# A new order for the weight sums, high parts and low parts of the second MLP product, and a fourth buffer for its raw weights

## The chip, the core and the metric

The kernel runs on one core of one Trainium2 chip. The metric is the device time of one execution in microseconds (us). The engines that matter here are TensorE (PE in the profile, with its weight loads listed as PEld), VectorE (DVE), ScalarE (ACT), GpSimd (POOL) and SyncE (SP). In this part of the kernel POOL and SP only issue transfers. Each engine takes its instructions in the order in which they stand in its queue; engines wait for each other through semaphores.

## The reference

The block is a linear-attention layer followed by an MLP over the tokens. Only the second half of the MLP is touched here:

```python
def _B_ref(x, w1, b1, w2, b2):
    h = _layernorm(x, axis=-1)                       # (B, S, D)
    u = jnp.einsum("bsd,sf->bdf", h, w1) + b1        # (B, D, F)
    u = _gelu(u)
    y = jnp.einsum("bdf,fs->bds", u, w2) + b2        # (B, D, S)
    return y.transpose(0, 2, 1)

x = A_x
h = x + _A_ref(_layernorm(x, axis=-1), A_wqkv, A_w_phi, A_wo)
h2 = h + _B_ref(_layernorm(h, axis=-1), B_w1, B_b1, B_w2, B_b2)
```

S = 2048 tokens, D = 512 channels, F = 1792 hidden units, everything in float32. The second product is `y = u @ w2`, with 1792 x 2048 weights.

## The kernel before

The kernel has four parts that overlap at their edges: projections of the attention, its output with the second layer norm, the first MLP product (weights w1, until about 386 us of the span), and the second MLP product (weights w2, from there to the end). The change is in the last part.

Float32 accuracy is reached by splitting every operand into a high part in the format float32r and a low part, which is the difference; a product is then high x high, high x low and low x high. To save products, the second MLP product goes over 2 x 2 blocks of the matrices and uses seven products of sums of blocks in place of eight (the scheme of Strassen and Winograd). The seven operands on the weights' side are w2's four blocks, of which one is overwritten by a sum, and three more sums; they lie in one raw tile of 7 x 256 columns (`wraw`), so that one instruction makes all seven high parts (`whi`, on ScalarE) and one all seven low parts (`wlo`, on VectorE).

The work is cut thus. The output has 16 tiles of 128 tokens, taken as 8 row pairs (`sp` 0 to 7). A row pair needs all 14 tiles of hidden units, taken as 7 pairs (`p` 0 to 6). One (sp, p) is a step, n = 7 sp + p; there are 56. Weights are loaded for `GRP` = 2 steps at a time: a group g holds steps 2g and 2g + 1, there are 28 groups (`NGR`), and a load is 512 KB. A group begins in the middle of a row pair when sp is odd, since 7 is odd.

The names used below, with their lines:

- S(g), the sums of group g (`sums_w2`, L773): it starts the load (L771, on SP's queue), makes the sums on VectorE (L782, L783, L784), and before the change also issues the high parts.
- H(g), the high parts: one ACTIVATE of 128 x 1792 on ScalarE (L785) from `wraw` into `whi`, which has 3 buffers, so H(g) waits until TensorE has finished group g - 3.
- L(g), the low parts (`lo_w2`, L787): one VectorE subtraction of 128 x 1792 (L794) into `wlo`, which has 2 buffers, so L(g) waits until TensorE has finished group g - 2. TensorE reads it first at the second matmul of group g (L810).
- The load of group g goes into one of 3 raw buffers, and so waits until L(g - 3) has read the old contents.
- C(sp), the combination at the end of a row pair (L846 to L873): the six PSUM banks of the row pair are put together into two output tiles by VectorE (L855 to L862) with four copies by ScalarE (`e` L852, `low` L854), and four accumulating transfers leave from POOL's queue (L866, L871, L872, L873). The last row pair has its own combination (L878 to L899).
- There are 8 PSUM banks. A row pair takes 6, in turn, so that its third to sixth banks are the ones that held the first to fourth bank of the row pair before; TensorE waits there until C has read them.

The last two steps of a row pair (p = 5 and 6) run as one block, bank by bank. In that block group g's second half is needed one step early when sp is even.

The order of PE, DVE and ACT in this part is the order of the program text (`manual_schedule`, L825); SP's and POOL's queues are ordered by the scheduler. Before the change, S and L are called in this order: ahead of the steps S(0), L(0), S(1); then at each even n with p < 6 one S and one L, S first; and at the end of an even row pair (n even, p = 6) one L between the first and second output tile of C, and one S after C. On VectorE this reads

```
row pair 0:  S2 L1  S3 L2  S4 L3  C0a L4 C0b S5
row pair 1:  S6 L5  S7 L6  S8 L7  C1
row pair 2:  S9 L8  S10 L9  S11 L10  C2a L11 C2b S12
```

and so on. The pool `hp` (L762) is opened on the place where the first product's weight buffers `wf` lay (L517: raw, high and low, four of each); before the change it holds only `hb`, two tiles of the last row pair that are read back from the output (L880).

Of the kernel before, what the change touches and what calls it, by code (L numbers as in the profile page):

```python
# [9 lines left out]
F32 = mybir.dt.float32  # L10
F32R = mybir.dt.float32r  # L11
AF = mybir.ActivationFunctionType
# [5 lines left out]
P = 128  # L18
# [6 lines left out]
GRP = 2  # L25
# [11 lines left out]
def block_kernel(ctx: ExitStack, tc: tile.TileContext, x, xT, wT, phic, wo, w1, b1, w2, b2,  # L37
                 kvmask, ident_in, out):
    nc = tc.nc
# [33 lines left out]
    sums = ps_s.tile([P, SUMS, NPR, 2, 2], F32, name="smq")  # L73
# [26 lines left out]
    def load_x(t):  # L100
        raw = kk.tile([P, KD, P], F32, name="xraw", bufs=3)
        nc.sync.dma_start(raw, xT[t])
        return raw
# [298 lines left out]
    for t in range(3, NT - 1):  # L402
        if t + 2 < NT:
            raw = load_x(t + 2)
# [310 lines left out]
    ws = ctx.enter_context(tc.tile_pool(name="ws", bufs=2, side="right", reuse_waits="tile"))  # L715
# [46 lines left out]
    hp = ctx.enter_context(tc.tile_pool(name="hp", bufs=1, reuse_waits="tile"))  # L762

    STEPS = [(sp, p) for sp in range(NT // 2) for p in range(NP)]
    NGR = len(STEPS) // GRP
    RAW, WH, AW = {}, {}, {}
    done = {"sums": 0, "lo": 0}

    def load_w2(g):
        RAW[g] = ws.tile([P, 7, GRP * P], F32, name="wraw", bufs=3)  # L770
        nc.sync.dma_start(RAW[g][:, 1:5], w2[g])  # L771

    def sums_w2():  # L773

        g = done["sums"]
        if g == NGR:
            return
        done["sums"] += 1
        load_w2(g)
        raw = RAW[g]  # L780
        WH[g] = ws.tile([P, 7, GRP * P], F32R, name="whi", bufs=3)
        nc.vector.tensor_add(raw[:, 0:2], raw[:, 1].unsqueeze(1).to_broadcast([P, 2, GRP * P]), raw[:, 2:4])  # L782
        nc.vector.tensor_add(raw[:, 5], raw[:, 1], raw[:, 2])  # L783
        nc.vector.tensor_add(raw[:, 6], raw[:, 4], raw[:, 5])  # L784
        nc.scalar.activation(WH[g], raw, AF.Copy)  # L785

    def lo_w2():  # L787

        g = done["lo"]
        if g == NGR:  # L790
            return
        done["lo"] += 1
        wl_ = ws.tile([P, 7, GRP * P], F32R, name="wlo", bufs=2)
        nc.vector.tensor_sub(wl_, RAW[g], WH[g])  # L794
        for i, step in enumerate(STEPS[g * GRP:(g + 1) * GRP]):
            AW[step] = WH[g][:, :, i * P:(i + 1) * P], wl_[:, :, i * P:(i + 1) * P]

    with tc.issue_after(LO[-18]), tc.issue_after(LD[-20]):
        sums_w2()
        lo_w2()  # L800
        sums_w2()

    PROD = ((2, 1, 0, None), (5, 5, 1, None), (0, 0, 2, 0), (1, 4, 2, 1), (3, 6, 3, None), (6, 2, 4, None),
            (4, 3, 5, None))
# [11 lines left out]
    def products(sp, ps, order):  # L816
        for a, b, bk, half in order:
            for p in ps:
                wh_, wl_ = AW[sp, p]
                product(bank[bk], half, (wh_[:, a], wl_[:, a]), UB[p, b], half != 1, p == 0, p == NP - 1)  # L820

    def flat(a):
        return a.rearrange("p k d -> p (k d)")
# [3 lines left out]
    for n, (sp, p) in enumerate(STEPS):  # L827
        t = 2 * sp
        last = t + 2 == NT
        if n % GRP == 0 and p < NP - 1:  # L830
            sums_w2()
            lo_w2()
        if p == 0:
            bank = []
            for _ in range(6):
                pool = (ps_f, ps_q, ps_b, ps_b)[n_bank % 8 // 2]
                bank.append(pool.tile([P, 2, HD], F32, name="py", tag="pu"))
                n_bank += 1
        order = LAST if last else PROD
        if p < NP - 2:  # L840
            products(sp, [p], order)
            continue
        if p < NP - 1:
            continue
        products(sp, [p - 1, p], order)
        e = uo.tile([P, 2, HD], F32, name="e")  # L846
        u2 = uo.tile([P, HD], F32, name="u2", bufs=1)
        u3 = uo.tile([P, HD], F32, name="u3")
        if not last:
            ot = uo.tile([P, 2, 2, HD], F32, name="ot", bufs=1)  # L850
            low = uo.tile([P, 3, HD], F32, name="low", bufs=1)
            nc.scalar.activation(e[:, 1], bank[0][:, 0], AF.Copy)  # L852
            for i in range(3):
                nc.scalar.activation(low[:, i], bank[3 + i][:, 1], AF.Copy)  # L854
            nc.vector.tensor_add(e[:, 1], bank[0][:, 1], e[:, 1])  # L855
            nc.vector.tensor_sub(u2, bank[1][:, 0], e[:, 1])
            nc.vector.tensor_add(u2, bank[1][:, 1], u2)
            nc.vector.tensor_sub(u3, u2, bank[2][:, 0])
            nc.vector.scalar_tensor_tensor(e[:, 0], bank[2][:, 1], -1.0, u2, op0=ALU.mult, op1=ALU.subtract)

            def out_block(i, h, o, add):
                nc.vector.scalar_tensor_tensor(ot[:, i, h], o, b2s[:, t + i:t + i + 1], add, op0=ALU.add, op1=ALU.add)  # L862

            out_block(0, 0, bank[2][:, 1], u3)
            out_block(0, 1, bank[3][:, 0], u3)
            nc.gpsimd.dma_start(out[t * P:(t + 1) * P, :], flat(ot[:, 0]), accum_op=ALU.add)  # L866
            if n % GRP == 0:
                lo_w2()
            out_block(1, 0, bank[4][:, 0], e[:, 0])
            out_block(1, 1, bank[5][:, 0], e[:, 1])  # L870
            nc.gpsimd.dma_start(out[(t + 1) * P:(t + 2) * P, :], flat(ot[:, 1]), accum_op=ALU.add)  # L871
            nc.gpsimd.dma_start(out[t * P:(t + 1) * P, HD:D], low[:, 0], accum_op=ALU.add)  # L872
            nc.gpsimd.dma_start(out[(t + 1) * P:(t + 2) * P, :], flat(low[:, 1:3]), accum_op=ALU.add)  # L873
            if n % GRP == 0:
                sums_w2()
            continue

        hb = [hp.tile([P, 2, HD], F32, name=f"hb{i}") for i in range(2)]  # L878
        for i in range(2):
            nc.sync.dma_start(flat(hb[i]), out[(t + i) * P:(t + i + 1) * P, :])  # L880
            nc.vector.tensor_scalar(hb[i], hb[i], b2s[:, t + i:t + i + 1], None, op0=ALU.add)
        nc.scalar.activation(e[:, 1], bank[0][:, 0], AF.Copy)
        nc.vector.tensor_add(e[:, 1], bank[0][:, 1], e[:, 1])
        nc.vector.tensor_add(hb[1][:, 1], e[:, 1], hb[1][:, 1])
        nc.vector.tensor_sub(u2, bank[1][:, 0], e[:, 1])
        nc.vector.tensor_add(u2, bank[1][:, 1], u2)
        nc.vector.tensor_sub(hb[1][:, 0], hb[1][:, 0], u2)
        nc.vector.tensor_sub(u3, u2, bank[2][:, 0])
        nc.vector.tensor_sub(hb[1][:, 0], hb[1][:, 0], bank[2][:, 1])
        nc.vector.tensor_add(hb[0], hb[0], u3.unsqueeze(1).to_broadcast([P, 2, HD]))  # L890
        nc.vector.tensor_add(hb[0][:, 0], bank[2][:, 1], hb[0][:, 0])
        nc.vector.tensor_add(hb[0][:, 1], bank[3][:, 0], hb[0][:, 1])
        nc.vector.tensor_add(hb[0][:, 1], bank[3][:, 1], hb[0][:, 1])
        nc.sync.dma_start(out[t * P:(t + 1) * P, :], flat(hb[0]))
        nc.vector.tensor_add(hb[1][:, 0], bank[4][:, 0], hb[1][:, 0])
        nc.vector.tensor_add(hb[1][:, 0], bank[4][:, 1], hb[1][:, 0])
        nc.scalar.dma_start(out[(t + 1) * P:NT * P, 0:HD], hb[1][:, 0])
        nc.vector.tensor_add(hb[1][:, 1], bank[5][:, 0], hb[1][:, 1])
        nc.sync.dma_start(out[(t + 1) * P:NT * P, HD:D], hb[1][:, 1])  # L899
# [49 lines left out]
```

## Time and profile before

| | |
|---|---|
| time, median of 3 runs | 537.56 us (537.2, 537.56, 539.2) |
| the profiled execution | 539.4 us, of which the span of the profile is 537.6 us |
| granted TensorE clock, mean | 0.999 |
| PE busy in the span | 521.9 us (97%) |
| DVE busy in the span | 394.8 us (73%) |
| ACT busy in the span | 278.4 us (52%) |
| stretch 386.5 to 533.0 us, 146.5 us: PE, DVE, ACT, POOL busy | 142.51, 120.73, 55.86, 24.62 us |

A row of the timeline gives start, duration, engine, line, operation, output <- inputs and shapes, and in brackets the idle time of that engine just before, with what ended it. A row of the waits gives the waiting instruction, what released it, the total in us, how many times, and the longest. The chain of waits is the path of work that ended last, followed back from the end; its rows give start, duration and what. Matmuls overlap in the pipeline, so that a matmul's own duration is longer than the distance to the next one; the distance is what counts.

### The profile page before, as it was taken

The numbers are of one execution on the slowest core, as the hardware profiler recorded it, in microseconds if no ns is written. First come the engines' busy times: TensorE is split into PE (matmuls) and PEld (weight loads), VectorE is DVE, ScalarE is ACT, GpSimd is POOL, SyncE is SP. The second block draws the span as 40 slices with busy tenths as digits, with TensorE's granted clock in tenths as the row PEclk, the third lists the DMA queues.
The fourth block names the chain that finished last, engine by engine and source line by source line (L and its number), as shares of the span: only waits on it lengthen the run. The fifth ranks groups of instructions, "written<-read, shape, count | busy, mean of one in ns | idle before, by whom it ended". The sixth has DMA issues, their size and how long they took to land.

```text
span 537.6 us, 8845 instructions
## 1 busy us (share of the span) xinstructions
PE 521.9 (97%) x3343; PEld 433.8 (81%) x3343; DVE 394.8 (73%) x684; ACT 278.4 (52%) x481; POOL 247.2 (46%) x204
## 2 busy tenths in 40 slices
PE   8999999999999989999999999999999899999996
PEld 7888888886877757778788888888898788888885
DVE  6993999877699989874326426527668878888885
ACT  6998744434337766557755434425534334435330
POOL 2589699876889988886425000000002111211210
PEclk9999999999999999999999999999999999999999
DMA  8534300020502333434333463532027568667752
GB/s 307 191 121 118 98 21 21 1 80 1 159 1 78 99 102 94 119 114 123 98 99 98 117 215 99 177 97 62 20 79 134 127 152 175 139 147 176 146 90 59
DMA packets 36298, 58.52 MB, mean 109 GB/s; under 512 B 3744, under 2 KB 19360, under 8 KB 36256
## 3 DMA queue, kind: packets, MB, share of 16 engines
q1 hardware_dynamic: 31936, 51.37, 30.8%
q0 software_dynamic: 4032, 6.42, 9.5%
q8 instruction: 26, 0.43, 0.4%
q10 hardware_dynamic: 288, 0.17, 0.1%
q14 instruction: 16, 0.13, 0.1%
HBM read 46.81 MB, written 11.14 MB: 108 GB/s over the span
## 4 chain that ended last, share of the span: by engine, by line
PE 57%; DVE 15%; POOL 12%; DMA 6%; ACT 5%; issue 3%; SPq 0%; DVEq 0%; POOLq 0%; ACTq 0%
PE pu L65 10%; PE pu L66 10%; PE pu L67 10%; DMA wraw<-in_w 5%; POOL ez L445 4%; DVE wlo L794 4%; POOL eq L463 3%; PE py L809 3%; PE pv L66 2%; PE pv L67 2%; PE pv L65 2%; PE pk_ps L65 2%; PE pk_ps L66 2%; PE pk_ps L67 2%; PE py L813 2%
## 5 line engine op out<-in xcount | busy, mean ns | idle before, releaser
L66 PE MATMUL pu<-hs,whi 128*128 128x512 f32 x224 | 87.6, 391 | 2.2 <-POOL hs L61 2.2
L604 DVE TENSOR_TENSOR wlo<-wraw,whi 128x512 fp32r<-128x512 f32 x56 | 50.7, 910 | 51.5 <-ACT whi L612 50.4
L65 PE MATMUL pu<-hs,whi 128*128 128x512 f32 x224 | 87.4, 395 | 0.0
L67 PE MATMUL pu<-hs,wlo 128*128 128x512 f32 x224 | 87.0, 390 | 0.0
L866 POOL DMA_DIRECT2D out<-ot x7 | 6.2, 891 | 167.2 <-DVE ot L862 167.2
L785 ACT ACTIVATE whi<-wraw 128x1792 fp32r<-128x1792 f32 x28 | 47.1, 1701 | 62.7 <-DVE wraw L784 53.1
L809 PE MATMUL py<-uf,whi 128*128 128x512 f32 x195 | 71.2, 398 | 0.0
L794 DVE TENSOR_TENSOR wlo<-wraw,whi 128x1792 fp32r<-128x1792 f32 x28 | 56.4, 2021 | 4.5 <-PE py L810 2.2
L612 ACT ACTIVATE whi<-wraw 128x512 fp32r<-128x512 f32 x56 | 34.8, 625 | 46.9 <-PE pu L66 43.2
L810 PE MATMUL py<-uf,wlo 128*128 128x256 f32 x195 | 55.9, 287 | 3.2 <-DVE wlo L794 3.1
L66 PEld LDWEIGHTS pu<-hs,whi 128*128 128x128 f32 x224 | 42.1, 188 | 11.5 <-POOL hs L61 3.2
L65 PEld LDWEIGHTS pu<-hs,whi 128*128 128x128 f32 x224 | 42.1, 188 | 10.8 <-issue 2.5
L67 PEld LDWEIGHTS pu<-hs,wlo 128*128 128x128 f32 x224 | 42.0, 188 | 9.1 <-DVE wlo L604 0.4
L809 PEld LDWEIGHTS py<-uf,whi 128*128 128x128 f32 x195 | 36.8, 189 | 6.9
L445 POOL TENSOR_TENSOR ez<-eq,zB 128x1024 f32<-128x1024 f32 x16 | 40.9, 2561 | 2.5 <-ACT zB L491 2.5
L810 PEld LDWEIGHTS py<-uf,wlo 128*128 128x128 f32 x195 | 36.9, 189 | 6.4 <-DVE wlo L794 6.4
L198 POOL TENSOR_TENSOR pk<-pk,sk 128x1024 f32<-128x1024 f32 x16 | 31.0, 1943 | 9.8 <-DVE sk L197 9.0
L463 POOL TENSOR_TENSOR eq<-eq,w 128x1024 f32<-128x1024 f32 x16 | 32.0, 1998 | 4.0 <-DVE w L460 4.0
L813 PE MATMUL py<-uf,whi 128*128 128x256 f32 x170 | 32.0, 282 | 0.0
L202 POOL TENSOR_TENSOR zacc<-zacc,pk 128x1024 f32<-128x1024 f32 x13 | 31.2, 2401 | 0.6
L809 PE MATMUL py<-un,whi 128*128 128x512 f32 x78 | 29.0, 401 | 0.7 <-DVE ot L862 0.6
L61 POOL TENSOR_TENSOR hs<-hn,hs 128x512 fp32r<-128x512 f32 x16 | 21.5, 1342 | 17.8 <-ACT hs L60 17.8
(183 smaller groups left out, 1319.3 us busy)
## 6 DMA issues: line engine op xcount, KB each, us to landing
wraw<-in_w SPq DMA_DIRECT2D x56, 256.0 KB, 2.8
wraw<-in_w SPq DMA_DIRECT2D x28, 512.0 KB, 4.4
xraw<-in_xT SPq DMA_DIRECT2D x16, 256.0 KB, 3.1
xh<-in_x SPq DMA_DIRECT2D x16, 256.0 KB, 2.7
h<-in_x SPq DMA_DIRECT2D x16, 256.0 KB, 2.8
out<-h SPq DMA_DIRECT2D x16, 256.0 KB, 3.0
out<-ot POOLq DMA_DIRECT2D x14, 256.0 KB, 4.5
wraw<-in_wT SPq DMA_DIRECT2D x12, 256.0 KB, 5.0
```

The costliest lines, as they stand in the source:

```text
L65: nc.tensor.matmul(o, ah, bh, start=first, stop=False)
L66: nc.tensor.matmul(o, ah, bl, start=False, stop=False)
L67: nc.tensor.matmul(o, al, bh, start=False, stop=last)
L445: nc.gpsimd.tensor_mul(EZ[t], EQ[t], zB)
L463: nc.gpsimd.tensor_mul(heads(EQ[t]), heads(EQ[t]), W[t].rearrange("p g c h -> p (g c h)").unsqueeze(2).to_broadcast([P, 2 * H, DH]))
L604: LO.append(nc.vector.tensor_sub(wl_, raw, wh_).ins)
L612: nc.scalar.activation(wh_, raw, AF.Copy)
L785: nc.scalar.activation(WH[g], raw, AF.Copy)
L794: nc.vector.tensor_sub(wl_, RAW[g], WH[g])
L809: nc.tensor.matmul(o, a[0], b, start=start, stop=stop, skip_group_check=True)
L810: nc.tensor.matmul(o[:, 0], a[1], b[:, 0], start=False, stop=stop, skip_group_check=True)
L813: nc.tensor.matmul(o[:, half], a[x], b[:, y], start=start and first and i == 0, stop=stop and i == 2, skip_group_check=True)
```

## The change

The sums, the high parts and the low parts become three functions, called in a new order and with new distances. Ahead of the steps there are now three S, two H and one L. At each even n with p < 6 the order is L, H, S in place of S (with its H), L. In the middle of the combination of an even row pair an H follows the L; the S after it stays. On VectorE this reads

```
row pair 0:  L1 S3  L2 S4  L3 S5  C0a L4 C0b S6
row pair 1:  L5 S7  L6 S8  L7 S9  C1
row pair 2:  L8 S10  L9 S11  L10 S12  C2a L11 C2b S13
```

The raw tiles get names of their own, one buffer each, and a fourth one in the pool `hp`. Groups 0 to 3 use slots 0, 1, 2, 0; from group 4 on the slots go 3, 1, 2, 0 in turn. The load of group g waits from then on for L(g - 4). `hb` lies behind the new buffer in `hp`.

```diff
@@ -764,10 +764,11 @@
     RAW, WH, AW = {}, {}, {}
-    done = {"sums": 0, "lo": 0}
+    done = {"sums": 0, "hi": 0, "lo": 0}
 
     def load_w2(g):
-        RAW[g] = ws.tile([P, 7, GRP * P], F32, name="wraw", bufs=3)
+        slot = g % 3 if g < 4 else (3, 1, 2, 0)[g % 4]
+        RAW[g] = (hp if slot == 3 else ws).tile([P, 7, GRP * P], F32, name=f"wraw{slot}", tag=f"wraw{slot}", bufs=1)
         nc.sync.dma_start(RAW[g][:, 1:5], w2[g])
 
     def sums_w2():
@@ -778,11 +779,18 @@
         done["sums"] += 1
         load_w2(g)
         raw = RAW[g]
-        WH[g] = ws.tile([P, 7, GRP * P], F32R, name="whi", bufs=3)
         nc.vector.tensor_add(raw[:, 0:2], raw[:, 1].unsqueeze(1).to_broadcast([P, 2, GRP * P]), raw[:, 2:4])
         nc.vector.tensor_add(raw[:, 5], raw[:, 1], raw[:, 2])
         nc.vector.tensor_add(raw[:, 6], raw[:, 4], raw[:, 5])
-        nc.scalar.activation(WH[g], raw, AF.Copy)
+
+    def hi_w2():
+
+        g = done["hi"]
+        if g == NGR:
+            return
+        done["hi"] += 1
+        WH[g] = ws.tile([P, 7, GRP * P], F32R, name="whi", bufs=3)
+        nc.scalar.activation(WH[g], RAW[g], AF.Copy)
 
@@ -796,9 +804,12 @@
     with tc.issue_after(LO[-18]), tc.issue_after(LD[-20]):
-        sums_w2()
-        lo_w2()
-        sums_w2()
+        for i in range(3):
+            sums_w2()
+            if i < 2:
+                hi_w2()
+            if i < 1:
+                lo_w2()
 
@@ -828,8 +839,9 @@
         if n % GRP == 0 and p < NP - 1:
+            lo_w2()
+            hi_w2()
             sums_w2()
-            lo_w2()
         if p == 0:
@@ -866,6 +878,7 @@
             if n % GRP == 0:
                 lo_w2()
+                hi_w2()
             out_block(1, 0, bank[4][:, 0], e[:, 0])
```

## The prediction

> **What bounds the kernel now.** I read the page first (TensorE is busy for 97% of the span), then the chain of waits, to see how regularly TensorE advances through the second product, then the table of waits of that stretch, and last the timelines of VectorE, ScalarE and TensorE around the places where it doesn't.
>
> The page's head and its transfers, then the chain of waits (start, duration, what):
>
> ```profile
> span 537.6 us, 8845 instructions
> ...
> out<-ot POOLq DMA_DIRECT2D x14, 256.0 KB, 4.5
> ...
> out<-low POOLq DMA_DIRECT2D x7, 256.0 KB, 6.1
> ```
>
> ```profile
> 387.20 0.72 PE py L813 x6
> ...
> 397.14 0.71 PE py L813 x6
> ...
> 523.61 0.71 PE py L813 x6
> ...
> 529.05 0.44 DVE e L883
> ...
> 534.07 0.42 DVE hb L896
> ```
>
> The six L813 matmuls stand at the same place in every single step. Those of step 0 begin at 387.20, those of step 4 at 397.14: (397.14 - 387.20) / 4 = 2.485 us a step, undisturbed. Those at 523.61 are step 52's. Undisturbed they would come at 387.20 + 52 x 2.485 = 516.42. So TensorE loses 7.19 us in the product, and this is all that an order of the other engines can win there. From 529.05 on the chain is VectorE without a pause, the last combination; it keeps its length.
>
> The waits from 350 us on, and TensorE's timeline at three of the losses:
>
> ```profile
> DVE wraw L782 <- DMA wraw<-in_w: 8.8, 6, 2.9
> PEld py L810 <- DVE wlo L794: 6.4, 10, 1.2
> ...
> PE py L810 <- DVE wlo L794: 3.1, 9, 0.9
> ...
> PEld py L809 <- DVE ot L862: 0.9, 1, 0.9
> ...
> PE py L809 <- DVE ot L862: 0.6, 1, 0.6
> ```
>
> ```profile
> 411.75 0.38 PE L810 MATMUL py<-uf,wlo 128*128 128x256 f32 x1 [0.17 <-DVE wlo L794]
> ...
> 424.55 0.51 PE L809 MATMUL py<-un,whi 128*128 128x512 f32 x1 [0.57 <-DVE ot L862]
> ...
> 429.18 0.39 PE L810 MATMUL py<-uf,wlo 128*128 128x256 f32 x1 [0.91 <-DVE wlo L794]
> ```
>
> Ten times TensorE waits for a late low part, once for a PSUM bank that the combination had not read. (PE and PEld rows of one wait overlap; they aren't added.) Around 424.55, start-to-start distances beyond the normal ones sum to about 1.3 us, which leaves 7.2 - 1.3 = 5.9 us for the ten low parts.
>
> Why they are late, by VectorE's timeline of 396 to 430 us:
>
> ```profile
> 396.54 2.03 DVE L794 TENSOR_TENSOR wlo<-wraw,whi 128x1792 fp32r<-128x1792 f32 x1 [1.50 <-PE py L810]
> ...
> 403.57 2.02 DVE L794 TENSOR_TENSOR wlo<-wraw,whi 128x1792 fp32r<-128x1792 f32 x1 [0.16 <-PE py L810]
> ...
> 406.30 0.68 DVE L782 TENSOR_TENSOR wraw<-wraw 128x512 f32<-128x512 f32 x1
> ...
> 407.82 0.68 DVE L782 TENSOR_TENSOR wraw<-wraw 128x512 f32<-128x512 f32 x1
> ...
> 409.67 2.02 DVE L794 TENSOR_TENSOR wlo<-wraw,whi 128x1792 fp32r<-128x1792 f32 x1 [0.25 <-ACT whi L785]
> ...
> 418.04 0.69 DVE L782 TENSOR_TENSOR wraw<-wraw 128x512 f32<-128x512 f32 x1 [2.89 <-DMA wraw<-in_w]
> ...
> 419.57 2.02 DVE L794 TENSOR_TENSOR wlo<-wraw,whi 128x1792 fp32r<-128x1792 f32 x1
> 421.83 0.42 DVE L855 TENSOR_TENSOR e<-py,e 128x256 f32<-128x256 f32 x1 [0.24 <-ACT e L852]
> ...
> 425.59 0.68 DVE L782 TENSOR_TENSOR wraw<-wraw 128x512 f32<-128x512 f32 x1
> ...
> 427.11 2.02 DVE L794 TENSOR_TENSOR wlo<-wraw,whi 128x1792 fp32r<-128x1792 f32 x1
> 429.04 0.69 DVE L782 TENSOR_TENSOR wraw<-wraw 128x512 f32<-128x512 f32 x1
> ```
>
> From starts: S costs 427.11 - 425.59 = 1.52 us, L 429.04 - 427.11 = 1.93, C 425.59 - 421.83 = 3.76. After row pair 0 two sums (S5 at 406.30, S6 at 407.82) stand ahead of L5, which ends at 411.69; TensorE gets on at 411.75. Before row pair 1's end S8 sits 2.89 us waiting for its load; L7 and C1 are late behind it, the bank is late (424.55), and S9 stands ahead of L8, which ends at 429.13 (TensorE: 429.18). All ten have one of these shapes.
>
> **The change part by part.** *The order on VectorE.* The same instructions run; against the L's, each S moves one place. Two row pairs hold 7 S, 7 L and 2 C, 7 x 3.45 + 2 x 3.76 = 31.7 us, against 14 x 2.485 = 34.8 us of TensorE, so 3.1 us may be idle.
>
> After an even row pair: L4 at 403.57, the rest of C0, S6 from 406.30 to 407.82, then L5 at once, to 409.84: 1.9 us ahead of the 411.75 at which it was taken late, or 1.4 ahead of the 411.3 at which it was wanted. Gain 0.44 there, and the same at its later copies.
>
> At an odd row pair: L3 started at 396.54, 0.60 before step 4's L813, when its buffer was released; L7 in its turn can start 0.60 before step 12's, which without new losses is 387.20 + 12 x 2.485 = 417.02, or 417.46 with the 0.44 already lost: at 416.86, not 419.57. Then S9, and C1 starts at 416.86 + 1.93 + 1.52 = 420.31. The trace's C1 began at 421.83 and cost 1.3 us in banks, so the latest free start is about 420.5: 0.2 us to spare. C1 ends at 424.07, L8 at 426.1; step 16's first L810 is wanted at about 426.8. Spare 0.7.
>
> In the middle of an even row pair (L3, L10, L17, L24) the low part then starts at its release, as L3 did at 396.54, and TensorE lost nothing there.
>
> So the ten waits (-5.9) and the bank's (-1.3) both go. The thinnest spot is the bank: S9 now stands ahead of C1. What it costs, at three odd row pairs (the last has another combination), lies between 0 and 3 x 1.3 = 3.9 us; I take 0.5, near the lower end, since the worked start is early.
>
> *ScalarE.* No instruction is added. H now follows the L of its turn in the text, and its sums were made a turn earlier, so it no longer waits for them (409.67's cause) but only for its buffer. What queues behind it is the copy `e` for C; at the odd row pairs H can end 416.9 + 1.7, two microseconds ahead of C1. Zero.
>
> *Loads.* Their landing, and the rows for the place of the fourth buffer (SP's and TensorE's timelines):
>
> ```profile
> DMA to landing us min/median/max: 3.1/4.4/6.6
> ```
>
> ```profile
> 368.89 8.55 SPq L880 DMA_DIRECT2D hb<-out  x2
> ```
>
> ```profile
> 386.34 0.39 PE L67 MATMUL pu<-hs,wlo 128*128 128x512 f32 x1
> ```
>
> Before, one S and one L (3.45 us) lie at the least between the release of a raw buffer and the sums on its new contents, less than a median landing of 4.4. After, two of each do, 6.9 us, more than the longest landing of 6.6. So the 8.8 us of waits at L782 go; their worth is in the terms above.
>
> The Trainium skill, "DMA: Bandwidth & Descriptors", section "Anatomy of one DMA — SWDGE (gpsimd) path", fits 2.0 us plus the bytes at 436 GB/s, on a POOL queue: an estimate of 3.2 us for these 512 KB. By it three buffers would do, the same sum would come from the order alone, and the late-load rival below would have no chance. The trace disagrees (4.4 median on SP's queue, 2.89 us waited), and its rows are used.
>
> The first load into the new place waits for w1's buffers: at the latest the last w1 matmul, 386.34 + 0.39. It lands by 386.7 + 6.6 = 393.3; S4 comes after L2, at 393.4 in the old trace. `hb`, moved behind it, may hold SP's queue as long, no longer. If that place were released only when the first product's operands are all made, some 4 us later, S4 would wait 4 us and L3, with 1 us to spare, would be 1.5 to 3 us late, once. I take 0, with 3 as the upper end.
>
> *Ahead of the steps.* By the stretches, 310 to 386.5 us:
>
> ```profile
> 310.00:386.50 76.50, 76.50 (x339) 63.36 (x338) 38.79 (x75) 32.59 (x59) 0.00 (x0) 1.00 0.39 117
> ```
>
> TensorE has no hole here, VectorE is half idle (38.79 of 76.50), and the same four S, two L and three H run early as before. Zero; if the cover failed, one S, 1.5 us, would be late, once.
>
> Sum: -5.9 - 1.3 + 0.5 = -6.7 us. Against the profiled execution's own 539.4 us (537.6 of span and 1.8 around it) that is 532.7; it was 1.84 us above the median of the runs, so for the median 537.56 - 6.7 = **530.9 us**.
>
> **The rivals.** *The bank stays late.* The low parts come on time but C1, C3 and C5 start as late as C1 did, behind one S more: -7.2 + 3.9 = -3.3, 534.3 us. For it: 0.2 us to spare. Against it: the wait for the load, 2.89 us, made C1 late, and that goes.
>
> *The output transfers become the bound.* POOL's timeline of row pair 0:
>
> ```profile
> 403.74 1.06 POOL L866 DMA_DIRECT2D out<-ot  x1 [111.62 <-DVE ot L862]
> ...
> 414.21 0.86 POOL L873 DMA_DIRECT2D out<-low  x1 [3.92 <-DMA out<-ot]
> ```
>
> L873 leaves at 414.21 and lands some 6.1 later, at 420.3: 16.6 us after the first issue, when a row pair would take 7 x 2.485 = 17.4. `low` has one buffer. If faster loads slow these transfers by a few us, ScalarE's copies wait, and H behind them; the pitch stays near the present (523.61 - 387.20) / 52 x 7 = 18.4 us: no change, 537.5 us. Against it: the next writer of that part, row pair 1's last copies, is wanted at about 420.4 and nothing hangs on it at once. In this form the change would not do what it says.
>
> *Late loads in front of the combination*, the slower side. S5, S9, S12 and so on now stand ahead of a C; where such a load is late, banks and the next L wait with it. At the three odd row pairs everything beyond 0.2 us is lost on TensorE. To be 2.7 us slower than before, these must take back 7.2 and cost 2.7 more, 3.3 each: S9's load would land 3.5 us after S9's turn. Its buffer is free at 409.84, its turn is 418.79, so the landing would have to be 12.4 us. From 9.2 us on it costs anything. Price at 12.4: 540.3 us. Against it: no landing over 6.6.
>
> **How the numbers follow.** A measurement of this kernel can tell about 0.5%, 2.7 us, from no change. Forecast 0.74; bank late 0.14; output transfers 0.06; late loads 0.06. The forecast's own range is 530.0 (nothing left of the 7.2, less 0.4 of scatter) to 533.9 (3 us at the fourth buffer). To hold 8 in 10 it takes in the bank's rival, whose terms lie anywhere up to 3.9: **529.7 to 535.5**. Faster by over 0.5% (below 534.9) are the forecast and over half of the bank's cases, 0.82; within, 0.11; slower, 0.07.
>
> **What would show it.** Right: the L813 at step 52 stand some 136.4 - 6.7 = 129.7 us after step 0's; the waits of PE and PEld on `wlo` L794 are gone; L782 no longer waits for its load; C1 starts after S9 without waiting for ScalarE. A wait of L809 on `ot` in odd row pairs shows the bank; of `low` L854 on a transfer, the outputs; of L782 on the load just ahead of L855, late loads. The forecast is wrong if TensorE has a loss of over 1 us in each row pair, whoever causes it.

## The result, and the profile after

| | before | after |
|---|---|---|
| median time | 537.38 us (4 runs, 536.79 to 539.2) | 532.29 us (4 runs, 531.65 to 532.76) |
| profiled execution | 539.4 us, span 537.6 | 532.09 us, span 530.3 |

The medians differ by 5.1 us, 0.95%; the ratio of the mean times is 0.9899, with a 95% interval of 0.9873 to 0.9925, so the kernel is faster. Forecast were 530.9 us, in a range of 529.7 to 535.5. A second set of runs of the same two kernels gave 531.94 against 537.45 us, 0.9891 (0.9868 to 0.9914).

The engines' shares of the chain of waits before, then the page after, its head and the same shares:

```profile
PE 57%; DVE 15%; POOL 12%; DMA 6%; ACT 5%; issue 3%; SPq 0%; DVEq 0%; POOLq 0%; ACTq 0%
```

```profile
span 530.3 us, 8842 instructions
...
PE 518.7 (98%) x3343; PEld 433.9 (82%) x3343; DVE 394.0 (74%) x684; ACT 278.0 (52%) x481; POOL 246.7 (47%) x204
...
PE 82%; POOL 10%; DVE 4%; ACT 2%; DMA 1%; issue 1%; SPq 0%; DVEq 0%; POOLq 0%; ACTq 0%
```

VectorE is as busy as before (394.0 us, and 394.8 then), but its share of the chain has gone from 15% to 4%; TensorE's has gone from 57% to 82%. The chain of waits after, at the rows that were read before (L824 is the old L813, L909 the old L896):

```profile
386.98 0.72 PE py L824 x6
...
516.30 0.71 PE py L824 x6
...
526.76 0.42 DVE hb L909
```

Those two L824 rows are steps 0 and 52: 516.30 - 386.98 = 129.32 us, 2.487 a step, which is the undisturbed pitch. The distance was 136.41. All of the 7.19 us lost there in the profiled execution before are gone but 0.1. The span is 7.3 us shorter; the other 0.2 us lie ahead of step 0, and the tail behind is as long as it was.

In the table of waits of the second product after, no row has TensorE or its weight loads waiting for VectorE, and none has L782 waiting for a load. What is left are waits that cost nothing:

```profile
ACT low L866 <- PE py L821: 13.2, 15, 2.5
DVE wlo L802 <- PE py L821: 8.8, 9, 1.5
```

The wait has turned round. Before, TensorE waited ten times for a low part; now the low part (L802) waits nine times for TensorE to release its buffer. VectorE's timeline after, at the first odd row pair:

```profile
416.21 2.03 DVE L802 TENSOR_TENSOR wlo<-wraw,whi 128x1792 fp32r<-128x1792 f32 x1 [1.42 <-PE py L821]
418.15 0.68 DVE L782 TENSOR_TENSOR wraw<-wraw 128x512 f32<-128x512 f32 x1
...
419.68 0.42 DVE L867 TENSOR_TENSOR e<-py,e 128x256 f32<-128x256 f32 x1
...
423.42 2.02 DVE L802 TENSOR_TENSOR wlo<-wraw,whi 128x1792 fp32r<-128x1792 f32 x1
```

L7 starts when its buffer is free, S9 stands behind it with its load landed (at 415.87, 2.3 us before its turn), and C1 and L8 follow without a hole. Against the working of the prediction: L7 was to come 0.60 us before the place of step 12's L824 at the undisturbed pitch, and that place is 386.98 + 12 x 2.487 = 416.82, so it came 0.61 before; C1 was to come 2.85 us after that place, and came 2.86 after.

### The profile page after: what moved, and what is told of

It reads as the page before. It is cut to its first block, busy times and chain, and to the rows that moved or that the text cites. A ratio compares the mean times of both kernels' runs of the same rounds, so it can differ in the third digit from the quotient of the medians.

```text
span 530.3 us, 8842 instructions
## 1 busy us (share of the span) xinstructions
PE 518.7 (98%) x3343; PEld 433.9 (82%) x3343; DVE 394.0 (74%) x684; ACT 278.0 (52%) x481; POOL 246.7 (47%) x204
## 4 chain that ended last, share of the span: by engine, by line
PE 82%; POOL 10%; DVE 4%; ACT 2%; DMA 1%; issue 1%; SPq 0%; DVEq 0%; POOLq 0%; ACTq 0%
PE py L820 12%; PE pu L65 11%; PE pu L66 11%; PE pu L67 11%; PE py L824 8%; PE py L821 6%; POOL ez L445 4%; POOL eq L463 3%; PE pv L66 2%; PE pv L67 2%; PE pv L65 2%; PE pk_ps L65 2%; PE pk_ps L67 2%; PE pk_ps L66 2%; POOL hs L61 2%; PE po L65 1%
## 5 line engine op out<-in xcount | busy, mean ns | idle before, releaser
L802 DVE TENSOR_TENSOR wlo<-wraw,whi 128x1792 fp32r<-128x1792 f32 x28 | 56.5, 2022 | 12.0 <-PE py L821 8.8
L824 PE MATMUL py<-uf,whi 128*128 128x256 f32 x170 | 32.0, 283 | 0.0
```

What stands on the lines that cost most here:

```text
L824: nc.tensor.matmul(o[:, half], a[x], b[:, y], start=start and first and i == 0, stop=stop and i == 2, skip_group_check=True)
```

## The experiments

The experiments ran on three chips. The kernel before, run beside them on each, had medians of 537.36 to 537.64 us, so the times are compared as they stand.

**The two kernels again.** The profiled execution before, at 539.4 us, was 2 us over its median, so each kernel was profiled once more.

> The changed kernel again, for a second profile and a tighter ratio. Theory: TensorE has no loss left in the second product, so that the distance from step 0's L824 to step 52's is 129.3 us again, and the time is 532.3 us, 0.990 of before. Rival (the first profile was a lucky one): some L820 or L821 wait on ot or wlo again, distance over 130 us.

> The kernel before again, for the spans of several executions and a second profile. Theory: the losses of TensorE in the second product change from execution to execution with the landing of the loads, and the first profile (539.4 us against a median of 537.4) had about 2 us more of them than the middle: an execution of 537.4 us has about 5.2 us of loss between step 0's L813 and step 52's (distance 134.4 us against 136.4). Rival: the loss is 7.2 us in every execution and the 2 us lie elsewhere, in the earlier stages or outside the span.

The kernel after has again no wait of TensorE, the distance is 129.3 us again, and its time is 531.94 us. The kernel before (0.9993 of itself, 0.9978 to 1.0008) was now profiled in an execution of 537.5 us, close to its median. Its chain and its waits:

```profile
387.81 0.72 PE py L813 x6
...
521.73 0.71 PE py L813 x6
```

```profile
DVE wraw L782 <- DMA wraw<-in_w: 6.3, 6, 1.3
PEld py L810 <- DVE wlo L794: 5.2, 10, 0.8
...
PE py L810 <- DVE wlo L794: 2.0, 8, 0.5
```

The distance is 133.92 us, the loss 133.92 - 129.22 = 4.7 us and not 7.2 (the theory had 5.2). The row of the bank is missing altogether, and the longest wait for a load is 1.3 us in place of 2.9. Behind the first odd row pair TensorE lost 2.5 us in the first profile and 0.8 in this one; behind the even ones, where no load is waited for, 0.4 to 0.5 in both. So the theory holds as far as two profiles go: what the old kernel loses moves with its waits for loads, and the first profile had shown a costly execution. The old order with four buffers, below, bears it out: it has no such wait, and its six runs lie within 0.9 us. It also ties up with the medians: 4.7 us of loss, 5.1 to 5.5 us won.

**One half of the change at a time.** First the new order without the fourth buffer:

```diff
-        slot = g % 3 if g < 4 else (3, 1, 2, 0)[g % 4]
+        slot = g % 3
```

> The new order with three raw buffers instead of four. The load of a group is then released by the low part three groups back, one turn (4.97 us) or, behind a combination, 4.2 us before its sums are wanted, against a landing of 4.3 us in the middle and 6.4 at most. Theory (order and buffer both count): VectorE waits at L782 again, up to 1.5 us ahead of C at odd row pairs, and TensorE loses 1 to 3 us of the 7.1 won: 533 to 535 us. Rival 1 (the order alone does it): 532.3 us, no wait on L782. Rival 2 (the early loads are all of it): 537 us.

Measured: 535.78 us, 0.9966 of before (0.9949 to 0.9983), 3.8 us over the kernel after. Waits and VectorE's timeline:

```profile
DVE wraw L782 <- DMA wraw<-in_w: 13.0, 9, 2.4
```

```profile
415.20 0.69 DVE L782 TENSOR_TENSOR wraw<-wraw 128x512 f32<-128x512 f32 x1 [1.72 <-DMA wraw<-in_w]
```

The loads are late again, nine times and 13.0 us, more than before the change (8.8): S8 here waits 1.72 us, and L7 and C1 behind it are late. The waits of TensorE:

```profile
PEld py L821 <- DVE wlo L802: 2.8, 3, 1.2
...
PE py L821 <- DVE wlo L802: 1.8, 3, 0.9
PEld py L820 <- DVE ot L874: 1.4, 3, 0.7
```

The order alone keeps a third of the gain. The theory named the mechanism, the late load, and was 0.8 us short in size. It had looked ahead of C at the odd row pairs, where the bank is late three times (the row of `ot`); the larger part, 2.6 of the 3.9 us lost, is three low parts in the middle of even row pairs, each behind the next late load (TensorE gets on at 435.09, 471.39 and 507.41 us).

Then the fourth buffer with the old order (the new `load_w2` in the kernel before, nothing else):

```diff
-        RAW[g] = ws.tile([P, 7, GRP * P], F32, name="wraw", bufs=3)
+        slot = g % 3 if g < 4 else (3, 1, 2, 0)[g % 4]
+        RAW[g] = (hp if slot == 3 else ws).tile([P, 7, GRP * P], F32, name=f"wraw{slot}", tag=f"wraw{slot}", bufs=1)
```

> The old order (S then L) with four raw buffers. Theory: no wait for loads is left, so C of odd row pairs and the low part behind it are in time; but at even row pairs S5, S6 still stand ahead of L5, and the high parts behind S5: four losses of about 0.45 us, 1.8 in all, 533.5 us, 0.993 of before. Rival (the order is the gain, the buffer nothing): 537 us, losses as before.

Measured: 533.95 us, 0.9928 of before (0.9908 to 0.9949). No wait for a load is left; the low parts are late four times, at 411.4, 446.7, 482.0 and 517.3 us, behind every even row pair. ScalarE's and VectorE's timelines at the first:

```profile
407.62 3.29 ACT L786 ACTIVATE whi<-wraw 128x1792 fp32r<-128x1792 f32 x2 [3.63 <-DVE wraw L785]
```

```profile
409.36 2.03 DVE L795 TENSOR_TENSOR wlo<-wraw,whi 128x1792 fp32r<-128x1792 f32 x1 [0.25 <-ACT whi L786]
```

H5 waits for S5, which stands behind C0, and L5 waits for H5 and for S6 ahead of it on VectorE; H5 ends last, by 0.25 us. That is worth 533.95 - 531.94 = 2.0 us. So the buffer, put in first, brings 3.5 of the 5.5 us, and the order the last 2.0; the other way round, the order brings 1.7 and the buffer 3.8.

**The order inside a turn, with four buffers.** Sums first again, all else as after:

```diff
-            lo_w2()
-            hi_w2()
             sums_w2()
+            lo_w2()
+            hi_w2()
```

> The changed kernel (four buffers, sums three ahead, high parts two ahead) with the sums called ahead of the low part again. A load then has one sum and one low part to land, 3.45 us at the least and 5 in an undisturbed turn, since the low part that frees the buffer now comes later by one place. Theory: VectorE waits at L782 again, in front of the low part, and TensorE loses 1 to 3 us: 533.3 to 535.3 us. Rival (the order inside a turn does not matter once there are four buffers): 532.3 us, no wait at L782.

Measured: 536.18 us, 0.9975 of before (0.996 to 0.9989), 0.9 us beyond the theory's range. VectorE's timeline shows S9 ahead of L7:

```profile
417.26 0.69 DVE L782 TENSOR_TENSOR wraw<-wraw 128x512 f32<-128x512 f32 x1 [2.75 <-DMA wraw<-in_w]
418.79 2.02 DVE L802 TENSOR_TENSOR wlo<-wraw,whi 128x1792 fp32r<-128x1792 f32 x1
```

With the sums three ahead, the load for S(g) waits for L(g - 4). Called first, S comes one sum and one low part sooner after that release, and four buffers are then worth no more than the three of the new order were (535.78 us). With the sums three ahead, "low part first" is what turns the fourth buffer into time for the load; with the sums two ahead, as in the run before this one, the fourth buffer gives that time in the old order too.

**The distances.** The kernel before with L and S changed round and nothing else: low part first, sums two ahead, three buffers.

```diff
-            sums_w2()
             lo_w2()
+            sums_w2()
```

> Low part first, but the sums only two groups ahead with their high part behind them, and three raw buffers. Each load still has two sums and two low parts (6.9 us) to land, since the low part now stands before the load it releases. Theory: no wait on L782; at even row pairs L5 waits for the high part of S5, behind the combination, 0 to 0.4 us of loss at four places, 0 to 1.6 us in all: 532.3 to 534 us. Rival (the third group ahead and the fourth buffer are needed): losses of over 3 us, 535.5 us or more.

Measured: 568.63 us, 1.0572 of before (1.0547 to 1.0596). The theory fell; its rival had the direction (535.5 us or more), but not the size or the cause. The loads are in time (no wait at L782), but the timelines of VectorE and ScalarE show a ring:

```profile
391.34 2.03 DVE L794 TENSOR_TENSOR wlo<-wraw,whi 128x1792 fp32r<-128x1792 f32 x1
393.28 0.68 DVE L782 TENSOR_TENSOR wraw<-wraw 128x512 f32<-128x512 f32 x1
...
396.71 2.03 DVE L794 TENSOR_TENSOR wlo<-wraw,whi 128x1792 fp32r<-128x1792 f32 x1 [1.83 <-ACT whi L785]
```

```profile
394.97 1.70 ACT L785 ACTIVATE whi<-wraw 128x1792 fp32r<-128x1792 f32 x1 [4.76 <-DVE wraw L784]
```

L2, behind it S3, behind it H3 on the other engine, behind it L3: 396.71 - 391.34 = 5.37 us a turn, where TensorE needs 4.97. Two engines that are each idle for part of the time make a chain that is longer than the turn. The copy `e` of each combination stands behind such an H too. With the sums three ahead and the high parts two, S, H and L of one turn belong to three different groups, and the ring is open.

From step 0's first L813 at 386.88 to step 52's at 552.14 it is 165.3 us, against 129.3 in the kernel after: TensorE loses 36 us. Not all of it is waiting; a part is TensorE's clock. Its timeline at the second combination, and the stretch behind (the column before the DMA share is the granted clock):

```profile
428.43 0.50 PE L813 MATMUL py<-un,whi 128*128 128x256 f32 x2 [3.38 <-DVE e L855]
```

```profile
429.45:436.20 6.75, 6.51 (x21) 5.45 (x22) 5.71 (x10) 0.88 (x1) 2.27 (x3) 0.50 0.54 73
```

After a hole of 3.4 us for a bank, TensorE runs at half its clock for 6.8 us, from 429.4 to 436.2. This happens at three of the seven combinations. TensorE is busy there for 6.5, 6.3 and 6.5 us, and the half of that, some 10 us, is an estimate of what the clock costs; the other 26 us are waits for low parts and banks.

The high parts three ahead, called behind their sums, in the kernel after (the part at the even steps is shown; ahead of the steps there are three H, and the H in the middle of a combination moves behind the S at its end):

```diff
             lo_w2()
-            hi_w2()
             sums_w2()
+            hi_w2()
```

> The changed kernel with the high parts three groups ahead, right behind their sums, instead of two. The buffer of H(g+3) is that of group g, so in the turn in which TensorE begins group g, ScalarE stands before H(g+3) until TensorE has ended it, and the copy e for the combination stands behind. Theory: C starts only 1.7 + 0.4 us after the end of each row pair instead of 1.5 us before it, so TensorE loses 3 to 4 us at each of seven row pairs, and its clock falls where a hole is over 3.4 us, as it did with the low part first and the sums two ahead: 555 to 575 us. Rival (the distance of the high parts does not matter, ScalarE is half idle): 532.3 us.

Measured: 565.54 us, 1.0529 of before (1.0501 to 1.0557), within the theory's range. TensorE's waits, and ScalarE's timeline at the end of row pair 0:

```profile
PE py L823 <- DVE e L866: 10.7, 7, 1.7
...
PE py L819 <- DVE ot L873: 3.6, 7, 0.6
```

```profile
403.63 1.70 ACT L793 ACTIVATE whi<-wraw 128x1792 fp32r<-128x1792 f32 x1 [5.40 <-PE py L819]
405.24 0.36 ACT L863 ACTIVATE e<-py 128x256 f32<-128x256 f32 x1
```

H waits 5.40 us for its buffer, and `e`, which only needs the first bank, stands behind it. C0 starts at 405.63; in the kernel after it starts at 399.86. TensorE loses 4.2 us there with its clock at 1.00, a little over the 3 to 4 expected. On the clock the theory named the effect and had its condition wrong: it tied the fall to a hole of over 3.4 us, no single wait of the matmuls here is longer than 1.7, and the clock fell at five of the seven places all the same. That the time lies in the range is in part luck. So high parts three ahead do not fit three buffers, and two do; one ahead was not tried.

**How much room the combination has.** The prediction's thinnest spot was C at the odd row pairs, 0.2 us. In the kernel after, k additions of 128x256 into a scratch tile were put ahead of C at row pairs 1, 3 and 5:

```diff
+        if not last and n % GRP:
+            for _ in range(k):
+                nc.vector.tensor_add(u3.rearrange("p (a b) -> p a b", b=P), ident.unsqueeze(1).to_broadcast([P, 2, P]),
+                                     ones.unsqueeze(1).to_broadcast([P, 2, P]))
```

> The changed kernel with one VectorE addition of 128x256 (about 0.35 us) more ahead of the combination of each odd row pair but the last (three places). Theory: 0.2 us are to spare at the fifth bank, so 0.1 to 0.2 us are lost at each, under 0.6 us in all, and the waits show L820 behind ot. Rival (there is more room than worked out): no wait of TensorE.

> The same with four such additions, 1.4 us, about as late as C1 was before the change. Theory: 1.4 - 0.2 = 1.2 us lost at each of three places, 3.6 us in all, about 535.9 us. Rival (more room than worked out): 1 us or less in all.

> The changed kernel with eight additions of 128x256 (0.43 us each, 3.4 us) ahead of the combination at three odd row pairs. Four of them cost 4.7 us in all. Theory: TensorE loses 3.4 - 0.24 = 3.2 us at each place, 9.6 in all, 541.6 us, in several holes of which the longest is about 2 us, so its granted clock stays at 1.0. Rival: the clock falls here too, 547 us or more.

> The same with twelve additions, 5.1 us. Theory: 5.1 - 0.24 = 4.9 us at each of three places, 14.7 in all, and now the longest hole is about 3.7 us, as long as the 3.5 us behind which the clock fell to half for some 6 us with the low part first and the sums two ahead; that is about 3 us more at each place: 556 us. Rival (the clock falls for another reason): 547 us with the granted clock at 1.0.

| additions | delay of C1, us | lost by TensorE at the three places, us | time, us |
|---|---|---|---|
| 0 | 0 | 0, 0, 0 | 531.94 |
| 1 | 0.34 | 0.17, 0.17, 0.17 | 532.55 |
| 4 | 1.71 | 1.53, 1.54, 1.53 | 536.96 |
| 8 | 3.55 | 4.7, 3.4, 4.9 | 544.81 |
| 12 | 5.38 | 5.9, 6.0, 7.6 | 552.1 |

The delay is read from VectorE's timeline, from the start of the first addition to that of C1; for four it is from 419.30 to 421.01. (The additions take 0.43 us each in a row and not 0.35, which is why four cost more than the 1.2 us a place of the theory.) The loss is what the start-to-start distances of the steps gained behind each place. The waits for one and for four:

```profile
PEld py L820 <- DVE ot L878: 0.6, 3, 0.2
```

```profile
PEld py L820 <- DVE ot L878: 2.7, 3, 0.9
...
PEld py L824 <- DVE e L871: 1.2, 3, 0.4
```

0.34 - 0.17 = 0.17 and 1.71 - 1.53 = 0.18; with eight, at the second place, 3.55 - 3.38 = 0.17. The room is 0.2 us, as worked out, and beyond it every delay is paid in full. At the other places of eight, and at all of twelve, more is paid than the delay. With eight, the theory had the clock at 1.0; it fell at just these two of the three places, and the time lies between the theory's 541.6 and the rival's 547. The stretches at the first place, and at the second, where it did not fall:

```profile
421.00:425.00 4.00, 1.98 (x11) 1.40 (x11) 3.62 (x10) 1.97 (x2) 0.00 (x0) 1.00 0.06 23
425.00:426.00 1.00, 0.43 (x3) 0.14 (x1) 1.00 (x4) 0.00 (x0) 0.00 (x0) 0.69 0.00 0
426.00:428.00 2.00, 2.00 (x7) 1.71 (x8) 2.00 (x4) 0.00 (x0) 1.51 (x2) 0.50 0.11 10
```

```profile
460.00:465.00 5.00, 2.73 (x15) 1.83 (x14) 4.59 (x12) 2.52 (x4) 0.00 (x0) 1.00 0.04 15
465.00:467.00 2.00, 1.68 (x10) 1.46 (x11) 2.00 (x5) 0.00 (x0) 1.05 (x2) 1.00 0.00 0
```

With twelve, the clock fell at all three places, and the time lies again between the two expectations (556 and 547): the direction of the theory, about half its size.

## Why the prediction was right, point by point

**What bounds the kernel.** Right in kind: the loss of TensorE in the second product was all there was to win, all but 0.2 us of the gain came from there, and the tail kept its length. The step that failed is the last of the sum: "against the profiled execution's own 539.4 us ... that is 532.7; it was 1.84 us above the median of the runs, so for the median 537.56 - 6.7". This took the whole 7.2 us of one execution, less 0.5 for the bank, off a median that does not hold them. The kernel after has no such loss to vary, and its eight runs spread over 1.1 us (531.65 to 532.76), where the kernel before spreads over 4.15 (535.4 to 539.55, 17 runs). The execution near the median that was profiled lost 4.7 us. With that term in place of 7.2, and nothing for the bank, the sum gives 537.4 - 4.7 = 532.7; measured were 532.3. Taken off the execution it was read from, the term was right: 539.4 - 7.2 = 532.2. The forecast was 1.4 us too low; that 532.3 lies in the range is owed to the room left for the bank and the fourth buffer, which cost nothing, and that part is luck: no term stood for how much the loss itself differs between executions.

**The two causes.** The prediction put S5 and S6 ahead of L5 (0.44 us at the even row pairs) beside the late loads (the odd row pairs). The old order with four buffers left just the first: 0.43 us at 411.4 and 0.5 at each of its three copies, 2.0 us of time. The new order with three buffers left the loads.

**The low parts at an odd row pair.** Right to 0.01 us in the start of L7 and of C1, seen above.

**The bank.** 0.5 us were set aside, and 0 were paid. The room of 0.2 us was worked out right and measured three times. So the rival in which the bank stays late was kept out by 0.2 us a place.

**ScalarE at zero, the fourth buffer's place at zero, the work ahead of the steps at zero.** All three right: no wait of TensorE has appeared, and S4, the first on the new place, starts right behind L2.

**The loads.** Right: two sums and two low parts between release and use hide a landing of 6.4 us at most; the closest load of the second product landed 1.6 us before its turn. The Trainium skill's fit for a transfer ("DMA: Bandwidth & Descriptors", section "Anatomy of one DMA — SWDGE (gpsimd) path"), which is for a POOL queue, gives an estimate of 3.2 us for these loads, and by it the fourth buffer would have been worthless. The old order with four buffers gained 3.5 us, and the loads land in 4.3 us (median after). The measurement decides.

**The output transfers.** They touch, as the rival said, and it costs nothing. The waits after:

```profile
ACT low L866 <- DMA out<-low: 4.2, 2, 2.2
```

The copies `low` wait twice for the transfer of the row pair before, up to 2.2 us, and no bank is late by it.

**Late loads in front of the combination.** Did not occur with four buffers. With three, late loads are what the new order loses, a third of it in front of a combination.

What was not tried: a fifth raw buffer, the sums four ahead, and the high parts one ahead.

## What to carry to other kernels

When one engine's profile shows it waiting for another that is busy 80% of the time, look for the order and the buffer that make the second one late before looking for less work: here VectorE ran 684 instructions before and after. Lay out one period by hand, with starts from the trace, and follow every ring of hand-overs through the engines: here low part, sums and high part that wait for each other inside one turn made a ring of 5.37 us in a turn of 4.97, though each engine was idle for part of it. And a loss that hangs on transfers differs from execution to execution, so take its size from an execution near the median, not from whichever one was profiled.

## What the runs showed of the hardware

That TensorE's clock would come into it was not expected, since it is granted in full in the second product of both kernels. In the four runs with the longest waits (the two slow orders, eight and twelve additions) it fell to 0.50 thirteen times within the second product, eight times for 3.4 us and five times for 6.8. With eight additions, the first fall and the stretch behind it:

```profile
425.40:428.80 3.40, 2.94 (x10) 2.56 (x10) 3.40 (x6) 0.00 (x0) 1.74 (x2) 0.50 0.28 29
428.90:431.00 2.10, 2.10 (x15) 1.92 (x14) 1.73 (x5) 0.40 (x1) 0.20 (x1) 1.00 1.19 127
```

This did not take one long hole: with eight additions the longest is 1.9 us,

```profile
423.61 0.50 PE L824 MATMUL py<-un,whi 128*128 128x256 f32 x2 [1.91 <-DVE e L871]
```

and in the stretch from 421 to 425 us TensorE was still busy for 1.98 of 4.00. Within a run the falls begin whole multiples of 3.41 us apart: with eight additions at 425.4 and 503.9 us (23 times), with twelve at 425.8, 466.8 and 507.7 (12 times each). So the place of a hole against this 3.41 us raster seems to count, and not its length alone; what share of a window must be idle is not shown. The Trainium skill, "TensorE: Matmul & The Clock Gate", section "Part 1: The HAM clock gate (the "warmup" mystery)", has in its table of the two states the clock at half after one idle window of about 3.4 us, with a window that runs freely. The hole of 3.4 us is as long as that; the holes of 1.9 us are not covered by the table as it stands, though a free-running window fits the raster, and fits that two places of three fell and the third, with the same longest hole, did not. The losses of the kernel before, 0.3 to 1.3 us at a time, left the clock at 1.00 from 386 to 530 us.
